# Waits between GpSimd and VectorE, and constant products in TensorE's early idle time, in a recurrent-attention and gated-MLP kernel

## The chip, the cores and the metric

The kernel runs on one core of a Trainium2 chip. The metric is the device time of one execution in microseconds; the time of a kernel is the median of its runs. The profile is of one execution. Its span goes from the first to the last instruction of the program; the execution's own time is a little longer.

The engines are named as in the profile: PE is TensorE's matmul, PEld its weight load, DVE is VectorE, ACT is ScalarE, POOL is GpSimd, and SP is the queue that issues DMAs. Each engine works through a list of instructions of its own.

## The reference

Two stages, in float32. First a recurrent attention with a decaying state, for 4 sequences, 8 heads, 768 steps, 48 values a head:

```python
for t in range(S):
    kt, vt, rt, wt = (k[:, :, t], v[:, :, t], r[:, :, t], w[:, :, t])
    cur = np.einsum('bhd,bhe->bhde', u[None] * kt, vt)
    y[:, :, t] = np.einsum('bhd,bhde->bhe', rt, state + cur)
    state = wt[:, :, :, None] * state + np.einsum('bhd,bhe->bhde', kt, vt)
```

Then an MLP on the 384 columns that the heads make together, with a gate that mixes the steps:

```python
h = x @ w_in                                  # 384 -> 1024
h = 0.5 * h * (1.0 + np.tanh(c * (h + 0.044715 * h ** 3)))
u, v = (h[..., :d_ff // 2], h[..., d_ff // 2:])
v_n = (v - mu) / np.sqrt(var + 1e-06) * g_ln  # mean and variance of v's 512 columns
v_s = np.einsum('ts,bsd->btd', w_sg, v_n) + b_sg[None, :, None]
return (x + (u * v_s) @ w_out).astype(np.float32)
```

## The kernel before

**The attention** goes in 24 chunks (4 sequences of 6 chunks of 128 steps), each in two halves of 64 steps. For a chunk the kernel loads the decays W, K and R together (KR), V (vtok) and, from the fifth chunk on, K and R by steps (RK). VectorE makes running products of the decays from both ends (L465 the suffix products, L473 or L480 the prefix products), multiplies K (L505) and R (L482) with them, TensorE makes the scores K R (L563), VectorE puts them into a masked matrix (L640), TensorE transposes K (L609), makes the products K V (L570), and the outputs from scores and state (L586, L597). The state is carried on by L654, L663, L670 and L683. The term with u needs `own`, a number for each step and head. For the first four chunks TensorE makes it from an elementwise K R (L515, then L519 against `u_col`). For the others it comes from RK: L527 multiplies by u, L529 by the other half, and L532 on VectorE sums.

**The MLP** works on float32 matrices that are split in two parts of reduced length, so that each product is three (L840, L841, L842). The weights come as float64 words and are split on the chip: L989, L991, L995 and L997 on VectorE for `w_in` (tile `vn`) and `w_out` (tile `g`), and for the first six, TensorE adds what is left (L1001 to L1003) and ScalarE copies it out. `w_sg` comes as float32 and is split by a copy (`wsgh`) and L1038 (`wsgl`). v's statistics are small 128x1 operations (tile `st`, L865 to L873), among them a power on GpSimd (L871).

**The order.** All this is written as some hundred small generators. Each yields an `Op` with the engines that could take it and a cost on each; `Plan.run` places the ops one after another by readiness and rank, picks an engine for each, and then lets the generator write the instructions. So the order of every engine's instructions comes from the costs in the plan, not from the chip. The plan treats some operations as users of a port that VectorE and GpSimd share:

```python
def port(self, e):
    return e == "POOL" or e == "DVE" and self.two
```

and plans no two of them at the same time. That is a matter of the plan alone: on the chip an instruction waits only for its data, its buffers, and its own engine.

**What the steps touch.** `m_m` is the pool of PSUM buffers for TensorE's products (tiles `m_ps`, three of them, and later `resets`). `full`, a 128x128 matrix of ones in `junk`, is set early on by GpSimd; `ident` is the unit matrix in the tile `same`, which GpSimd writes as the last of its preparations. `e_own`, `rk` and the like are the events and buffers by which the plan strings ops together. The transfers are issued on SP's queue in the plan's order: a load that waits for its buffer holds up those behind it.

Of the kernel before, what the change touches and what calls it, by code (L numbers as in the profile page):

```python
# [45 lines left out]
               (0, "load_v"): -15.0}  # L46
COLD = 15.0
FETCH = (3.6, 32, 66)
STRETCH = 6
RESETS = 8  # L50
AHEAD = {"decays": -0.24, "decayed_k": -1.91, "own_weights": 0.42, "masked": 0.16, "state": -0.26, "decayed": 1.33,
# [46 lines left out]
class Event:  # L98
    t = None
# [36 lines left out]
class Plan:  # L136
# [4 lines left out]
    def __init__(self):  # L141
        self.engines = dict.fromkeys(("PE", "DVE", "ACT", "POOL", "SP"), 0.0)
        self.procs = []
        self.log = []
        self.dma = 0.0
        self.lanes = [0.0] * 8
        self.port = 0.0
        self.count = 0
        self.pe_last = self.pe_before = None
        self.pos, self.came = FETCH[2], [0.0, 0.0]  # L150

    def fetched(self, t, end, n):

# [30 lines left out]
    def run(self):  # L184
        while True:
            best = {}
            for p in self.procs:
                op = p[3]
                if any(e.t is None for e in op.after) or any(len(s.free) < op.take.count(s) for s in op.take):
                    continue  # L190
                ready = max([p[2]] + [e.t for e in op.after] + [s.since(op.take.count(s)) for s in op.take])
                _, t, e = min((s + self.cost(op, e, s) + BIAS.get(e, 0.0), s, e) for e in op.on
                              for s in (max(ready, self.engines[e], self.port if op.port(e) else 0.0,
                                        self.lanes[0] if op.kb is not None else 0.0),))
# [9 lines left out]
            t, e, p = pick  # L204
            op = p[3]
            op.e, op.end = e, t + self.cost(op, e, t)
            if e == "PE":
                op.end += self.fetched(t, op.end, op.n)
            self.engines[e] = op.end
            if e == "PE":  # L210
                self.pe_before, self.pe_last = self.pe_last, op
# [6 lines left out]
            else:  # L218
                op.seen = op.end + self.LAT.get(e, 0.2)
            op.got = [s.take() for s in op.take]  # L220
            for b in op.free:
                b.done(op.seen)
            if op.done is not None:
                op.done.t = op.seen
            if not op.apart:
                p[2] = op.seen
            self.log.append((t, op.end, e, p[0], p[1].__name__))
            self._next(p, op)
            if p[3] is None:
                self.procs.remove(p)  # L230
        assert not self.procs, [(p[0], p[1].__name__) for p in self.procs[:40]]
# [70 lines left out]
def rwkv_gmlp(ctx: ExitStack, tc: tile.TileContext, wpad, kr, vtok, ktok, vt, u, ucol, w_in, consts_, w_sgT, w_out, out):  # L302
    nc = tc.nc
# [101 lines left out]
    plan = Plan()  # L405
    plan.engines.update(DVE=2.0, POOL=3.5, ACT=2.1, SP=0.8)
    PLANS.append(plan)
    steps = [(b, g) for b in range(B) for g in range(NC)]
    N = len(steps)

# [97 lines left out]
    def own_weights(n):  # L508

        x = ch[n]  # L510
        if n < ON_PE["own"]:
            op = yield Op({"DVE": 0.6, "POOL": 1.25}, after=[x.e_KR], take=[s_rk], done=x.e_own, two=True)
            rk, = op.got
            t = rk.tile.rearrange("p a b -> p (a b)")[:, 0:NP * C]
            engine[op.e].tensor_tensor(t, x.K, x.R, ALU.mult)  # L515
            op = yield Op({"PE": 0.8}, small=True, after=[e_uc], take=[m_m], free=[rk], n=16)
            m, = op.got
            for p in range(NP):
                nc.tensor.matmul(m.tile[:, 0:H], t[:, p * C:(p + 1) * C], u_col[:, p], start=(p == 0),  # L519
                                 stop=(p == NP - 1))  # L520
            op = yield Op({"DVE": 0.15, "ACT": 0.2}, take=[s_own], free=[m])
            own, = op.got
            copy(op.e, own.tile, m.tile[:, 0:H])
        else:
            op = yield Op({"POOL": 1.05, "DVE": 0.48}, after=[x.e_RK, e_u], two=True)
            t = x.rk.tile
            engine[op.e].tensor_tensor(t[:, 0], t[:, 0], u_bc, ALU.mult)  # L527
            op = yield Op({"POOL": 1.05, "DVE": 0.48}, two=True)
            engine[op.e].tensor_tensor(t[:, 1], t[:, 1], t[:, 0], ALU.mult)  # L529
            op = yield Op({"DVE": 0.47}, free=[x.rk], take=[s_own])  # L530
            own, = op.got
            nc.vector.tensor_reduce(own.tile, t[:, 1].rearrange("p (h e) -> p h e", e=D), AX.X, ALU.add)  # L532
# [760 lines left out]
```

## Time and profile before

| | |
|---|---|
| median of 3 runs | 371.54 us (369.52 to 372.68) |
| the profiled execution | 372.92 us |
| its span | 371.2 us |
| mean granted clock of TensorE | 0.989 |
| PE busy | 345.1 us, 93% of the span, 4429 instructions |
| DVE busy | 284.7 us, 77%, 571 instructions |
| ACT busy | 199.6 us, 54%, 520 instructions |
| POOL busy | 103.3 us, 28%, 140 instructions |
| HBM over the span | 131 GB/s |

How to read it: a row of a timeline has the start in us from the span's start, the time in us, the engine, the line, the operation, what it writes and reads, and the number of instructions merged in the row. In square brackets is the idle time of the engine before it and what ended it. Matmuls of float32 data appear as two records each, and their ends are modelled, so neighbouring rows overlap a little. Where a range of the profile has a granted clock, it is the share of full speed that TensorE's clock was given.

### The profile page before, as it was taken

Reading aid. Unit: us, or ns where it says so; the run is one execution under the profiler, and the core shown is the slowest. Engines: PE = TensorE matmul, PEld = TensorE weight load, DVE = VectorE, ACT = ScalarE, POOL = GpSimd, SP = SyncE. Lnnn points to the kernel's source line nnn. Section 1 sums busy time; section 2 is a strip of 40 time slices with the busy share of each in tenths; the row PEclk is TensorE's granted clock in tenths of the full one; section 3 lists DMA queues with packets and bytes.
Section 4 is the critical chain, followed back from the end, with each engine's and each line's share of the span. In section 5 each row is a group of like instructions: output and inputs, shape, how many; then the busy total and the mean of one; then the engine's idle time right before and its main releaser. Section 6 shows DMA issues by size and latency. Waiting matters only on the chain.

```text
span 371.2 us, 10746 instructions
## 1 busy us (share of the span) xinstructions
PE 345.1 (93%) x4429; PEld 312.5 (84%) x4429; DVE 284.7 (77%) x571; ACT 199.6 (54%) x520; POOL 103.3 (28%) x140
## 2 busy tenths in 40 slices
PE   2899588899999999999999999999999999999991
PEld 2576367679999889989899988999999899999991
DVE  7997999999999999899999998545726354553350
ACT  2666567767644677687564577521256783521110
POOL 6221917045233564534122611121100120100000
PEclk9989999999999999999999999999999999999997
DMA  8889477542435826746346620120445431001002
GB/s 243 330 272 312 150 241 221 177 159 71 125 119 175 263 76 196 245 133 189 92 141 191 194 77 3 64 79 6 140 152 181 134 117 50 1 0 44 21 8 66
DMA packets 23432, 50.64 MB, mean 136 GB/s; under 512 B 3024, under 2 KB 11984, under 8 KB 23376
## 3 DMA queue, kind: packets, MB, share of 16 engines
q1 hardware_dynamic: 23376, 49.88, 42.2%
q8 instruction: 37, 0.61, 0.7%
q14 instruction: 19, 0.16, 0.1%
HBM read 43.97 MB, written 4.72 MB: 131 GB/s over the span
## 4 chain that ended last, share of the span: by engine, by line
PE 69%; DVE 22%; issue 3%; DMA 2%; ACT 2%; SPq 0%; DVEq 0%; ACTq 0%
PE m_ps L840 14%; PE m_ps L841 13%; PE m_ps L842 13%; PE resets L840 5%; PE resets L842 5%; PE resets L841 5%; PE a_ps L563 4%; PE y_ps L586 3%; PE y_ps L597 2%; DVE W L465 2%; PE y_ps L570 2%; DVE W L473 2%; DVE KR L505 2%; DVE a L640 1%; DMA W<-in_wpad 1%
## 5 line engine op out<-in xcount | busy, mean ns | idle before, releaser
L840 PE MATMUL m_ps<-wsgh,vn 128*128 128x384 f32 x144 | 49.4, 343 | 0.3 <-ACT u L896 0.3
L841 PE MATMUL m_ps<-wsgl,vn 128*128 128x384 f32 x144 | 48.4, 336 | 0.0
L842 PE MATMUL m_ps<-wsgh,vn 128*128 128x384 f32 x144 | 48.4, 336 | 0.0
L871 POOL TENSOR_TENSOR st<-st,mhalf 128x1 f32<-128x1 f32 x24 | 17.3, 721 | 76.4 <-DVE st L869 69.4
L491 ACT ACTIVATE junk<-W 128x1040 bf16<-128x1040 f32 x24 | 25.7, 1070 | 13.4 <-DVE W L480 5.2
L840 PEld LDWEIGHTS m_ps<-wsgh,vn 128*128 128x128 f32 x144 | 27.0, 188 | 1.6 <-ACT u L896 0.6
L840 PE MATMUL m_ps<-xT,winh 128*128 128x384 f32 x78 | 27.0, 346 | 0.6 <-ACT kt L309 0.6
L841 PEld LDWEIGHTS m_ps<-wsgl,vn 128*128 128x128 f32 x144 | 27.0, 188 | 0.5
L842 PEld LDWEIGHTS m_ps<-wsgh,vn 128*128 128x128 f32 x144 | 27.0, 187 | 0.0
L840 PE MATMUL m_ps<-g,wouth 128*128 128x384 f32 (+1 forms) x80 | 26.8, 335 | 0.0
L842 PE MATMUL m_ps<-g,woutl 128*128 128x384 f32 (+1 forms) x80 | 26.4, 330 | 0.0
L841 PE MATMUL m_ps<-g,wouth 128*128 128x384 f32 (+1 forms) x80 | 26.4, 330 | 0.0
L841 PE MATMUL m_ps<-xT,winh 128*128 128x384 f32 x78 | 26.2, 336 | 0.0
L842 PE MATMUL m_ps<-xT,winl 128*128 128x384 f32 x78 | 26.2, 336 | 0.0
L563 PE MATMUL a_ps<-KR 64*64 64x128 f32 (+1 forms) x768 | 22.9, 256 | 1.1 <-DVE S L654 1.0
L527 POOL TENSOR_TENSOR RK<-RK,flat 128x384 f32<-128x384 f32 x17 | 20.9, 1234 | 10.7 <-DVE resets L920 6.4
L922 ACT CAST g<-m_ps 128x384 fp32r<-128x384 f32 x24 | 11.4, 477 | 21.4 <-DVE m_ps L920 21.4
L586 PE MATMUL y_ps<-a,vtok 64*64 64x64 f32 x768 | 21.3, 224 | 1.1 <-DVE S L670 0.6
L842 PE MATMUL m_ps<-winh,xT 128*128 128x512 f32 x51 | 20.2, 396 | 2.3 <-ACT xT L309 2.3
L465 DVE TENSOR_TENSOR_SCAN W<-W,D 128x520 f32<-128x520 f32 x16 | 21.9, 1371 | 0.0
L586 PEld LDWEIGHTS y_ps<-a,vtok 64*64 64x64 f32 x768 | 16.1, 134 | 6.7 <-issue 3.6
L942 DVE TENSOR_TENSOR o<-m_ps,x 128x384 f32<-128x384 f32 (+1 forms) x20 | 10.4, 529 | 14.6 <-PE m_ps L842 10.3
(184 smaller groups left out, 1009.5 us busy)
## 6 DMA issues: line engine op xcount, KB each, us to landing
KR<-in_kr SPq DMA_DIRECT2D x24, 512.0 KB, 4.5
RK<-in_ktok SPq DMA_DIRECT2D x20, 384.0 KB, 3.6
W<-in_wpad SPq DMA_DIRECT2D x24, 260.5 KB, 3.0
vtok<-in_vtok SPq DMA_DIRECT2D x24, 192.0 KB, 3.4
out<-o SPq DMA_DIRECT2D x23, 192.0 KB, 1.9
vn<-in_w_in SPq DMA_DIRECT2D x6, 512.0 KB, 6.9
KR<-in_w_in SPq DMA_DIRECT2D x6, 512.0 KB, 4.3
g<-in_w_sgT SPq DMA_DIRECT2D x6, 384.0 KB, 5.4
```

The costliest lines, as they stand in the source:

```text
L465: nc.vector.tensor_tensor_scan(Suf[:, WL - 1:0:-1], W[:, WL - 1:0:-1], r_one if early else D1[:, WL - 1:0:-1], 0.0, ALU.mult, ALU.add)
L473: nc.vector.tensor_tensor_scan(W[:, at], W[:, at], r_two, 0.0, ALU.mult, ALU.add)
L491: nc.scalar.activation(junk.bitcast(BF16).rearrange("p (a x) -> p a x", a=2), both, AF.Square, accum_out=chk[:, n:n + 1])
L527: engine[op.e].tensor_tensor(t[:, 0], t[:, 0], u_bc, ALU.mult)
L563: nc.tensor.matmul(ps_[64 * c_:64 * c_ + 64, j, p * C:p * C + (2 * T if c_ < turn else T)], x.K[rows, at:at + T], r_, start=True, stop=True)
L586: m = nc.tensor.matmul(place(y, j, q, r, c_), x.V[64 * c_:64 * c_ + 64, h * D - up(p, j):h * D - up(p, j) + 64], x.a.tile[64 * c_:64 * c_ ...
L840: nc.tensor.matmul(ps, lh, rh, start=(i == 0), stop=False)
L841: nc.tensor.matmul(ps, lh, rl, start=False, stop=False)
L842: nc.tensor.matmul(ps, ll, rh, start=False, stop=(i == n - 1))
L871: nc.gpsimd.tensor_tensor(rstd, var, c.mhalf, ALU.pow)
L922: nc.scalar.copy(gh, ps)
L942: nc.vector.tensor_tensor(o.tile[:, 0:w], ps, h_.x.tile[:, i, at], ALU.add)
```

## The change

It has two parts.

**GpSimd waits.** When the plan has placed an op, `port_order` looks at what it wrote. For an op on VectorE it notes the last instruction and the planned end. For an op on GpSimd it adds, to the first instruction, a wait for the last VectorE op whose planned end is not later than this op's planned start. VectorE gets no wait for GpSimd.

**Constant products.** TensorE multiplies a 128x128 constant by itself into a part of an `m_ps` buffer that nobody reads: eleven times `full` before anything else; two times `ident` ahead of each of the four `own` products (L519); and, for each wait of TensorE of more than 0.4 us that the plan foresees before 80 us of its own time, as many as fit at 0.22 us each, if a buffer is free by the plan. The plan's clock for TensorE starts at 6.4 us, and the products take no time in it.

```diff
+WARM = (11, 80.0, 0.22)
...
+            gap = t - self.engines[e] if e == "PE" and t < WARM[1] else 0.0
             self.engines[e] = op.end
...
             op.got = [s.take() for s in op.take]
+            if gap > 0.4:
+                self.fill(t - gap, int((gap - 0.15) / WARM[2]))
...
+            n = self.traced()
             self._next(p, op)
+            self.behind(op, n, t)
...
+    def warm(on, n, ps_):
+
+        for _ in range(n):
+            nc.tensor.matmul(ps_[:, 0:128], on, on, start=True, stop=True)
+
+    def fill(t, n):
+
+        free = [x for at, x in m_m.free if at <= t]
+        if free:
+            warm(ident, n, free[0])
+
+    warm(full, WARM[0], m_m.free[0][1])
+    plan.fill = fill
+    plan.engines["PE"] = 6.4
...
+    def port_order(op, n, t):
+
+        ins = nc.cur_bb.bb.instructions[n:]
+        if op.e == "DVE":
+            last = [i for i in ins if i.engine == mybir.EngineType.DVE]
+            if last:
+                on_dve.append((op.end, last[-1]))
+        elif op.e == "POOL" and ins:
+            before = [i for end, i in on_dve if end <= t + 0.01]
+            if before:
+                tc.add_manual_dep(ins[0], before[-1].name, wait, reason="port order")
+
+    plan.traced, plan.behind = lambda: len(nc.cur_bb.bb.instructions), port_order
...
             op = yield Op({"PE": 0.8}, small=True, after=[e_uc], take=[m_m], free=[rk], n=16)
             m, = op.got
+            warm(ident, 2, m.tile)
```

In the built program the instructions of VectorE, ScalarE, SP and GpSimd stand in the same order as before, and TensorE's too, but for 40 constant products put in between. The line numbers of the changed file are higher by 40 or 41 in the main part: L1038 is L1079 there, L527 L568, L529 L570, L482 L522, L465 L505, L505 L545, L519 L560 and L1001 L1042. The constant products are L421.

GpSimd, before, from its first split of `w_sg` on; in brackets are the signals that each row waits for:

```order
L1038 TENSOR_TENSOR wsgl<-g_414,wsgh 128x2x384 [waits DMAHW1_49,Activation_49]
L865 TENSOR_SCALAR st_0_113<-st_0_113 128x1 [waits Activation_49]
L1038 TENSOR_TENSOR wsgl<-g_463,wsgh 128x2x384 [waits DMAHW3_49,Activation_49]
L527 TENSOR_TENSOR RK_0_88<-RK_0_88,flat 128x384 [waits DMAHW6_49,DMAHW1_49]
L529 TENSOR_TENSOR RK_0_88<-RK_0_88 128x384 [waits Pool_49]
L527 TENSOR_TENSOR RK_0_89<-RK_0_89,flat 128x384 [waits DMAHW7_49]
L529 TENSOR_TENSOR RK_0_89<-RK_0_89 128x384 [waits Pool_49]
```

and the same rows now:

```order
L1079 TENSOR_TENSOR wsgl<-g_446,wsgh 128x2x384 [waits DMAHW1_49,DVE_49,Activation_49]
L906 TENSOR_SCALAR st_0_113<-st_0_113 128x1 [waits DVE_49,Activation_49]
L1079 TENSOR_TENSOR wsgl<-g_495,wsgh 128x2x384 [waits DMAHW3_49,DVE_49,Activation_49]
L568 TENSOR_TENSOR RK_0_88<-RK_0_88,flat 128x384 [waits DMAHW6_49,DMAHW1_49,DVE_49]
L570 TENSOR_TENSOR RK_0_88<-RK_0_88 128x384 [waits DVE_49,Pool_49]
L568 TENSOR_TENSOR RK_0_89<-RK_0_89,flat 128x384 [waits DMAHW7_49,DVE_49]
L570 TENSOR_TENSOR RK_0_89<-RK_0_89 128x384 [waits DVE_49,Pool_49]
```

The rows stand as before; each now waits for VectorE (DVE_49) too. The values of that signal in the built program say for which operation. They are given by the line numbers of before: the first L1038 waits for VectorE's own L1038, the L865 for an L471 behind it, the second L1038 for the L482 at the top of the next piece, the first L527 for the first L471 in it, its L529 for the L505, the second L527 for the second L471, and its L529 for the L540.

VectorE's order from that L482 on, which is the same before and now (with the line numbers of before):

```order
L482 TENSOR_TENSOR KR_0_84<-KR_0_84,W_0_80 128x512
L465 SCALAR_TENSOR_TENSOR W_0_79<-W_0_79,resets 128x520
L471 RECIPROCAL resets<-W_0_79 128x4
L473 SCALAR_TENSOR_TENSOR W_0_79<-W_0_79,resets 128x260
L309 CAST winl<-m_ps_0_130 128x512
L505 TENSOR_TENSOR KR_0_81<-KR_0_81,W_0_79 128x512
L640 COPY_PREDICATED a_0_98<-mask,a_ps_0_128 128x512
L471 RECIPROCAL resets<-W_0_79 128x4
L473 SCALAR_TENSOR_TENSOR W_0_79<-W_0_79,resets 128x260
L532 TENSOR_REDUCE own_0_90<-RK_0_88 128x8
L309 COPY look_0_93<-y_ps_0_129 128x1
L482 TENSOR_TENSOR KR_0_81<-KR_0_81,W_0_79 128x512
```

`resets`, `a_ps`, `m_ps` and `y_ps` lie in PSUM, the rest in SBUF. Nothing moved here: the waits tie GpSimd to places in this order. The L540 follows the last row.

TensorE, before, from its start to the first of the `w_in` products:

```order
L519 MATMUL m_ps_0_130<-u_col,RK_0_88 128x8 x3
L609 MATMUL m_ps_0_131<-same,KR_0_81 128x128 [waits DMAHW1_49,Pool_49]
L609 MATMUL m_ps_0_131<-same,KR_0_81 128x128 x3
L519 MATMUL m_ps_0_132<-u_col,RK_0_89 128x8 [waits DVE_49]
L519 MATMUL m_ps_0_132<-u_col,RK_0_89 128x8 x3
L563 MATMUL a_ps_0_128<-KR_0_81 64x64 [waits DVE_49]
L563 MATMUL a_ps_0_128<-KR_0_81 64x64 x15
L609 MATMUL m_ps_0_131<-same,KR_0_82 128x128 [waits DMAHW4_49,DVE_49,Activation_49]
L609 MATMUL m_ps_0_131<-same,KR_0_82 128x128 x3
L1001 MATMUL m_ps_0_130<-vn_184,same 128x512 [waits DVE_49,Activation_49]
```

and now, from the L609 of the first chunk on:

```order
L650 MATMUL m_ps_0_131<-same,KR_0_81 128x128 x3
L421 MATMUL m_ps_0_132<-same 128x128 x2
L560 MATMUL m_ps_0_132<-u_col,RK_0_89 128x8 [waits DVE_49]
L560 MATMUL m_ps_0_132<-u_col,RK_0_89 128x8 x3
L604 MATMUL a_ps_0_128<-KR_0_81 64x64 [waits DVE_49]
L604 MATMUL a_ps_0_128<-KR_0_81 64x64 x15
L650 MATMUL m_ps_0_131<-same,KR_0_82 128x128 [waits DMAHW4_49,DVE_49,Activation_49]
L650 MATMUL m_ps_0_131<-same,KR_0_82 128x128 x3
L421 MATMUL m_ps_0_132<-same 128x128 [waits Activation_49]
L421 MATMUL m_ps_0_132<-same 128x128 x9
L1042 MATMUL m_ps_0_130<-vn_195,same 128x512 [waits DVE_49]
```

Two constant products stand ahead of the second `own` product, and ten between the second transposes and the first of the `w_in` products; sixteen more stand ahead of everything shown, and twelve come later: two ahead of each `own` product of the third and fourth chunk, then one, two and five in waits that the plan foresees.

More of the change, by code (lines that the diff above doesn't have):

```diff
@@ L150, in __init__ @@
         self.pos, self.came = FETCH[2], [0.0, 0.0]
+        self.fill = lambda t, n: None
+        self.behind = lambda op, n, t: None
+        self.traced = lambda: 0
     def fetched(self, t, end, n):
@@ L407, in rwkv_gmlp @@
     PLANS.append(plan)
+    def warm(on, n, ps_):
[8 more added lines that the diff above has]
+    plan.engines["PE"] = 6.4
+    wait = mybir.DependencyInfo(mybir.DependencyClass.Sync, mybir.DependencyReason.DATA)
+    on_dve = []
+    def port_order(op, n, t):
[9 more added lines that the diff above has]
+    plan.traced, plan.behind = lambda: len(nc.cur_bb.bb.instructions), port_order
     steps = [(b, g) for b in range(B) for g in range(NC)]
```

## The prediction

> **What bounds the kernel now.** I read the busy time of each engine by stage first, and cut the stages where the picture changes.
>
> ```profile
> 0.00:12.40 12.40, 5.67 (x52) 5.15 (x52) 9.66 (x21) 3.56 (x8) 7.31 (x32) 1.00 0.85 279
> 12.40:38.90 26.50, 24.22 (x390) 16.20 (x390) 24.27 (x49) 18.46 (x51) 7.05 (x9) 0.94 0.86 294
> 38.90:94.90 56.00, 48.12 (x662) 38.56 (x661) 55.79 (x106) 38.21 (x97) 25.01 (x28) 1.00 0.52 160
> 94.90:360.90 266.00, 264.76 (x3316) 250.42 (x3317) 193.72 (x396) 139.41 (x365) 63.97 (x73) 1.00 0.36 112
> ```
>
> The columns are the stretch, its length, busy us of PE, PEld, DVE, ACT and POOL, the granted clock, the DMA share and GB/s. From 94.9 us on PE is never idle for long (1.24 us of 266), so a faster VectorE is worth nothing there. From 38.9 to 94.9 VectorE is busy 55.79 of 56 us and PE is idle for 7.88 us: VectorE bounds that stage, and what it saves there PE can take, up to those 7.88 us. Before 38.9 both are nearly full, PE partly at half clock.
>
> Next I read VectorE's timeline for rows longer than other rows of the same line.
>
> ```profile
> 12.40 1.72 DVE L989 TENSOR_SCALAR vn<-vn 128x512 int32<-128x512 int32 x2
> 17.73 0.40 DVE L989 TENSOR_SCALAR vn<-vn 128x512 int32<-128x512 int32 x1
> 19.15 0.68 DVE L991 SCALAR_TENSOR_TENSOR vn<-vn,vn 128x512 int32<-128x512 int32 x1
> 20.02 0.42 DVE L995 TENSOR_SCALAR vn<-vn 128x512 int32<-128x512 int32 x1
> 22.93 0.68 DVE L997 SCALAR_TENSOR_TENSOR winl<-vn,vn 128x512 fp32r<-128x512 uint32 x1
> 25.41 0.35 DVE L663 TENSOR_TENSOR S<-S,pc 128x192 f32<-128x192 f32 x1
> ...
> 36.80 0.72 DVE L640 COPY_PREDICATED a<-mask,a_ps 128x512 f32<-128x512 uint8 x1
> 38.96 2.04 DVE L989 TENSOR_SCALAR vn<-vn 128x512 int32<-128x512 int32 x1
> 41.19 1.22 DVE L991 SCALAR_TENSOR_TENSOR vn<-vn,vn 128x512 int32<-128x512 int32 x1
> 42.33 1.14 DVE L663 TENSOR_TENSOR S<-S,pc 128x192 f32<-128x192 f32 x1
> 43.40 1.22 DVE L995 TENSOR_SCALAR vn<-vn 128x512 int32<-128x512 int32 x1
> 44.81 1.22 DVE L997 SCALAR_TENSOR_TENSOR winl<-vn,vn 128x512 fp32r<-128x512 uint32 x1
> 46.55 1.22 DVE L465 TENSOR_TENSOR_SCAN W<-W,resets 128x520 f32<-128x520 f32 x1
> 49.22 0.68 DVE L505 TENSOR_TENSOR KR<-KR,W 128x512 f32<-128x512 f32 x1
> ...
> 58.80 1.82 DVE L873 TENSOR_TENSOR st<-st 128x1 f32<-128x1 f32 x1
> 63.50 0.83 DVE L663 TENSOR_TENSOR S<-S,pc 128x192 f32<-128x192 f32 x1
> 64.25 1.48 DVE L882 TENSOR_TENSOR vn<-v,vn 128x512 fp32r<-128x512 f32 x1
> 66.59 0.68 DVE L882 TENSOR_TENSOR vn<-v,vn 128x512 fp32r<-128x512 f32 x1
> 72.03 0.15 DVE L873 TENSOR_TENSOR st<-st 128x1 f32<-128x1 f32 x1
> 75.44 0.54 DVE L1010 TENSOR_TENSOR woutl<-g 128x384 fp32r<-128x384 f32 x1
> 79.94 1.19 DVE L1010 TENSOR_TENSOR woutl<-g 128x384 fp32r<-128x384 f32 x1
> 92.59 0.98 DVE L873 TENSOR_TENSOR st<-st 128x1 f32<-128x1 f32 x1
> ```
>
> And GpSimd's timeline at the same moments.
>
> ```profile
> 12.56 1.28 POOL L482 TENSOR_TENSOR KR<-KR,W 128x512 f32<-128x512 f32 x1 [0.73 <-DVE W L473]
> 36.87 1.84 POOL L1038 TENSOR_TENSOR wsgl<-g,wsgh 128x768 fp32r<-128x768 f32 x1 [0.84 <-ACT wsgh L309]
> 38.87 1.85 POOL L1038 TENSOR_TENSOR wsgl<-g,wsgh 128x768 fp32r<-128x768 f32 x1
> 40.68 1.18 POOL L527 TENSOR_TENSOR RK<-RK,flat 128x384 f32<-128x384 f32 x1
> ...
> 88.33 3.24 POOL L869 TENSOR_SCALAR st<-st 128x1 f32<-128x1 f32 x1 [2.88 <-ACT junk L867]
> ```
>
> L989 takes 0.40 us alone and 2.04 us when it starts 0.09 us behind a 1.85 us GpSimd operation: it waits until that one is done. L991 at 41.19 ends at 42.41, which is its 0.68 us behind the L527 of GpSimd that ends at 41.86; the long rows after it each find the next RK product of GpSimd in their way. L640 at 36.80 reads its values from PSUM and ends at 37.52, while GpSimd's L1038 runs on to 38.71: it is not held up. The Trainium skill, "SBUF — State Buffer", section "Who interferes with whom", says the same: a VectorE operation with two SBUF inputs, or in a two-port mode, and a GpSimd operation that reads SBUF exclude each other, and the first to start keeps the port.
>
> **What the waits are worth.** They keep GpSimd from running ahead of the planned order, so that each of its long operations falls behind the VectorE operation that the plan put ahead of it, which is mostly followed by one that reads PSUM. The excess of the long rows, each against its short row: 1.0 us at 12.40 (the pair took 1.72, two apart overlapping 0.08 would take 0.72), then 1.64, 0.54, 0.79, 0.80, 0.54 and 1.67 up to 60.6 us (6.0 in all), then 0.48, 0.80, 0.65 and 0.83 (2.8).
>
> What comes back: the L482 of GpSimd (12.56) now waits for L997, which ended at 17.2 us, and stands beside L640 (0.72) and for some 0.6 us against the L989 behind it; net 0.4. The L1038 of 38.87 now waits for VectorE's L482, whose successor starts at 46.55; from there to L505 at 49.22 nothing reads two SBUF inputs, 2.67 us, in which 1.85 us fit. The L527 behind it starts at about 48.5, lasts about 1 us and meets L505: 0.5 back. The second L527 meets the next VectorE L482 (0.3), an L871 at 58 us another (0.3): net 4.9 of 6.0. For 62 to 95 us I take 0.4 back: net 2.4. VectorE's sum is 0.4 + 4.9 + 2.4 = 7.7 us. From 95 us on the same kind of saving lies under PE and counts as zero; its cover is PE's 264.76 us of work, and if PE ever waited there the saving would count for more, not less.
>
> What is queued behind a waiting GpSimd operation is GpSimd's own order. The four L527/L529 end at about 54.2 us on the old clock, just ahead of the L532 on VectorE that reads the last of them; I bound this at 0 to 0.3 us each time. L482 of GpSimd also frees the buffer of the fourth W load, and SP's queue has a vn load right behind it:
>
> ```profile
> 17.53 0.37 SPq L984 DMA_DIRECT2D vn<-in_w_in  x1
> 27.49 0.40 DVE L989 TENSOR_SCALAR vn<-vn 128x512 int32<-128x512 int32 x1
> vn<-in_w_in SPq DMA_DIRECT2D x6, 512.0 KB, 6.9
> ```
>
> Both move by about 1.5 us (GpSimd's end at 17.2 + 1.3 against 17.05). With the median of 6.9 us from issue to landing, the vn load is there at 25.9, and VectorE reads it at 27.49. So SP costs nothing.
>
> **What the constant matmuls cost and bring.** PE rows:
>
> ```profile
> 9.55 1.88 PE L519 MATMUL m_ps<-u_col,RK 128*128 128x8 f32 x8 [0.15 <-DVE RK L515]
> 14.87 2.04 PE L1001 MATMUL m_ps<-vn,same 128*128 128x512 f32 x2 [1.33 <-DVE vn L991]
> 21.51 1.95 PE L519 MATMUL m_ps<-u_col,RK 128*128 128x8 f32 x16
> 29.70 0.29 DVE L309 COPY y<-y_ps 128x128 f32<-128x128 f32 x1 [1.82 <-ACT x L309]
> 43.49 0.51 PE L842 MATMUL m_ps<-winh,xT 128*128 128x512 f32 x1 [2.30 <-ACT xT L309]
> 27.00:28.00 1.00, 1.00 (x10) 0.67 (x11) 0.89 (x2) 0.79 (x2) 0.33 (x1) 0.50 0.92 353
> ```
>
> No row has a plain 128x128 float32 product. By L519, which loads the same weights and has two records each, one costs 1.95/8 = 0.24 us at full clock and 1.88/4 = 0.47 at half; more columns cannot be cheaper, so I take 0.25 and 0.47 as the ends. The first eleven and the five behind them (16 x 0.47 = 7.5 us at most) lie in the 6.7 us that PE is idle in the first stage and run about 1 us into L519, whose own eight records then take about half: nothing lost. The ten ahead of the first L1001 cost 2.5 us warm against a wait that was 1.33 us with PE cold, and PE arrives there earlier when warm: nothing again, but 4.7 us if cold. The four ahead of the L519 group at 21.51 stand on PE's path: 1.0 us. What they bring is the clock: it was 0.50 from 25 to 28.5 us, and behind that VectorE sat idle for 1.82 us. At full clock the 3.4 us of work shrink by 1.7; less 1.0 for the four, 0.7 to 0.8 us net; bounds -1.0 (clock falls anyway) and +1.8 (the whole wait). I take +0.8, since the fall follows weight loads with hardly any product, and the four break that up. The five at 40.6 us lay in a wait of 2.30 us which ended on ScalarE's xT behind VectorE's late L991; with that gone they stand exposed, 1.2 us less 0.2: minus 1.0 on PE.
>
> The row at 27 us shows PE busy for the whole microsecond at half clock. The Trainium skill, "TensorE: Matmul & The Clock Gate", Part 1, has the clock fall after an idle window of about 3.4 us; the trace differs, since PE was busy when it fell. By the page's rule the four products would do nothing for the clock, and the sum would be 1.8 us worse.
>
> **The sum.** VectorE could be 7.7 + 0.8 = 8.5 us earlier at 95 us. PE has to follow with the same work: it can give its 7.88 us of idle time and 0.8 of clock, less 1.0 for the exposed five. Of the idle time I leave a quarter, 1.9 us, standing: a choice, because waits on ScalarE stay and handovers get tighter. So 7.9 - 1.9 - 1.0 + 0.8 = 5.8 us. The profiled execution took 372.92 us (span 371.2), 1.38 above the median of 371.54; 372.92 - 5.8 = 367.1 there, 365.7 for a median.
>
> **Rivals.** *PE has no room.* Once VectorE stops waiting, PE between 38.9 and 94.9 is 86% full in an order that is fixed, and half of its idle time stays. For it: windows where both are full. Against: the longest wait, 2.30 us, hangs on rows that shrink. Gain 2.5, so 369.0.
>
> *The products run cold.* If the clock falls before 13.5 us, the ten take 4.7 us, L1001 starts at 18.2 instead of 14.9, and VectorE stands still behind the products that follow on PE, 3.3 us less some slack, say 2.7; with another 1.0 at 21.5 the gain falls to 2: 369.5. Against: sixteen back to back just before.
>
> *GpSimd starves (the slower side).* VectorE's next operation starts at once, GpSimd's only after the signal; if VectorE reads SBUF pairs back to back, GpSimd gets nothing, as at 88.33, where 128x1 took 3.24 us. Place: the RK products ahead of an L532, three times before 95 us (46, 68, 92), and the L871 ahead of an L873 twice (72, 81). At 3.24 less some 0.2 for the work, five times, VectorE would stand for 15.2 us against 7.7 gained: 7.5 us net, 379.0. It decides against the change as soon as VectorE's waits for GpSimd before 95 us come to more than the 7.7. Against: the operation behind the awaited one mostly reads PSUM.
>
> *The waits bind nothing*: where the awaited operation is long done nothing changes, 371.5. Against: from 38.87 on they bind for 7 us and more.
>
> **Chances.** Forecast 0.55; no room 0.18; cold 0.10; binds nothing 0.04; starved 0.13. Within 1%, what a measurement can tell from no change, is 367.8 to 375.3; so faster 0.56, same 0.31, slower 0.13. The range goes from 362.5 (all idle time gone) to 372.0 and leaves out the starved case and a little below.
>
> **What would show it.** Right: L989, L991, L663, L995 and L997 at about 40 us back to 0.4, 0.7, 0.35, 0.4 and 0.7 us; L873 at 0.15; GpSimd's L1038 and L527 7 us later in VectorE's order; PE without the wait of 2.30 us; full clock before 10 us and through 25 to 28.5; PE full from 89 instead of 95 us. Wrong: VectorE waiting for POOL RK or st, PE idle shared out anew, or L1001 later than 15 us.

## The result, and the profile after

The changed kernel takes 360.97 us (median; 359.32 to 362.9) where the kernel before, beside it on the same chip, takes 372.3 (369.52 to 373.5): a ratio of 0.9705, 95% interval 0.9661 to 0.9748. Once more on another chip the ratio was 0.9737 (0.9705 to 0.9769). The gain is 10 to 11 us, about twice the 5.8 that were forecast, and 360.97 lies below the range. The profiled execution took 360.7 us (span 359.0). In the changed kernel every line of before stands 40 or 41 further down (L989 is L1030), and L421 is the constant product.

Busy time by stage of the changed kernel, in the columns of the prediction. VectorE and PE are some 8.4 us ahead at the end of the third stretch, so I cut there; the end of the last is moved by the 12.2 us of the whole span, of which PE's work has won 10.3, so it holds a little less of that work than before:

```profile
0.00:12.40 12.40, 9.45 (x88) 9.04 (x88) 8.77 (x18) 3.46 (x8) 7.30 (x32) 0.97 0.83 293
12.40:38.90 26.50, 26.20 (x471) 20.19 (x464) 25.82 (x54) 19.26 (x53) 7.10 (x9) 0.95 0.87 291
38.90:86.50 47.60, 47.23 (x625) 38.92 (x624) 47.26 (x104) 37.63 (x96) 17.39 (x26) 1.00 0.58 186
86.50:348.70 262.20, 261.96 (x3304) 248.16 (x3304) 188.84 (x394) 138.57 (x365) 56.03 (x74) 1.00 0.37 114
```

The third stretch lasted 56.00 us before and PE was idle for 7.88 of them. Now it lasts 47.60, PE is idle for 0.37 and VectorE for 0.34: both are full, PE with 1.27 us of constant products among its work. From 86.5 us on PE is idle for 0.24 us, where it was 1.24.

VectorE's timeline, the rows that were long:

```profile
37.91 0.40 DVE L1030 TENSOR_SCALAR vn<-vn 128x512 int32<-128x512 int32 x1
38.49 0.68 DVE L1032 SCALAR_TENSOR_TENSOR vn<-vn,vn 128x512 int32<-128x512 int32 x1
39.09 0.35 DVE L704 TENSOR_TENSOR S<-S,pc 128x192 f32<-128x192 f32 x1
39.36 0.42 DVE L1036 TENSOR_SCALAR vn<-vn 128x512 int32<-128x512 int32 x1
39.96 0.68 DVE L1038 SCALAR_TENSOR_TENSOR winl<-vn,vn 128x512 fp32r<-128x512 uint32 x1
...
54.08 0.15 DVE L914 TENSOR_TENSOR st<-st 128x1 f32<-128x1 f32 x1
...
57.51 0.68 DVE L923 TENSOR_TENSOR vn<-v,vn 128x512 fp32r<-128x512 f32 x1
```

and GpSimd's beside it:

```profile
35.96 1.84 POOL L1079 TENSOR_TENSOR wsgl<-g,wsgh 128x768 fp32r<-128x768 f32 x1 [0.99 <-ACT wsgh L318]
37.77 0.24 POOL L906 TENSOR_SCALAR st<-st 128x1 f32<-128x1 f32 x1
41.38 1.86 POOL L1079 TENSOR_TENSOR wsgl<-g,wsgh 128x768 fp32r<-128x768 f32 x1 [3.38 <-ACT y L318]
43.20 1.00 POOL L568 TENSOR_TENSOR RK<-RK,flat 128x384 f32<-128x384 f32 x1
44.90 1.00 POOL L570 TENSOR_TENSOR RK<-RK 128x384 f32<-128x384 f32 x1 [0.69 <-DVE KR L545]
```

The second wsgl product no longer follows the first. GpSimd waits for 3.38 us. (The row puts the end of this wait down to ScalarE's y; by the signals of the built program the product waits for VectorE's L522 as well, the L482 of before, which starts at 40.56 us and ends at 41.24, 0.14 us ahead of it.) So VectorE has the whole split of vn and the L704 in its midst (2.04, 1.22, 1.14, 1.22 and 1.22 us before) to itself at 0.40, 0.68, 0.35, 0.42 and 0.68, and L914 (L873 before) is back from 1.82 to 0.15. Neither engine pays: GpSimd's own rows shorten too, as the groups of before and after show:

```profile
L527 POOL TENSOR_TENSOR RK<-RK,flat 128x384 f32<-128x384 f32 x17 | 20.9, 1234 | 10.7 <-DVE resets L920 6.4 <-DMA RK<-in_ktok 3.6 <-DVE S L663 0.7
```

```profile
L568 POOL TENSOR_TENSOR RK<-RK,flat 128x384 f32<-128x384 f32 x17 | 17.1, 1011 | 34.0 <-DVE RK L570 5.8 <-DVE W L520 5.1 <-DVE st L906 4.5
```

What PE waited for in 38.9 to 94.9 us of the kernel before (us in total, times, longest):

```profile
PE m_ps L842 <- ACT xT L309: 2.3, 1, 2.3
PE a_ps L563 <- DVE S L654: 1.0, 1, 1.0
PE m_ps L1003 <- DVE winl L997: 1.0, 1, 1.0
PE m_ps L609 <- DVE KR L505: 1.0, 1, 1.0
PE y_ps L597 <- DVE look L309: 0.7, 1, 0.7
PE m_ps L840 <- ACT kt L309: 0.6, 1, 0.6
PE m_ps L840 <- ACT v L863: 0.5, 1, 0.5
PE y_ps L597 <- POOL wsgl L1038: 0.3, 1, 0.3
PE a_ps L570 <- DVE a L640: 0.3, 1, 0.3
```

Three of them are put down to ScalarE, and each of these hangs on VectorE one step further back. ScalarE's xT, for which PE waited longest, stood behind a copy that had itself waited for VectorE's late L991. These are ScalarE's rows before:

```profile
42.44 0.62 ACT L1014 CAST winh<-vn 128x512 fp32r<-128x512 f32 x1 [1.56 <-DVE vn L991]
42.96 0.47 ACT L309 CAST xT<-m_ps 128x384 fp32r<-128x384 f32 x1
```

In the changed kernel the copy starts at 39.73 us without a wait and xT at 40.25. The v at 71.71 us follows a copy that waited 1.00 us for a VectorE split (L991 of `w_out`), and the kt at 81.95 follows an L876 that waited 0.96 us for VectorE's L873.

And from 38.9 us to the end in the changed kernel:

```profile
PE a_ps L611 <- DVE a L681: 0.2, 1, 0.2
```

That is the whole list of the waits it shows there; its second profile shows three of 0.3 us from the same place on. The chain that ended last says the same, first of before, then of after:

```profile
PE 69%; DVE 22%; issue 3%; DMA 2%; ACT 2%; SPq 0%; DVEq 0%; ACTq 0%
```

```profile
PE 89%; DVE 4%; DMA 3%; ACT 1%; SPq 1%; issue 0%; DVEq 0%
```

**The leads.** To see where time is won I subtract, for an instruction at the same place in an engine's list, its start in a variant from its start in the kernel before. The table, worked out so from the timelines, holds the changed kernel (twice, one execution each) and the variants that are told of below. The column heads are the place in time of the kernel before; V is VectorE, P is PE.

```
                      V 38   P 41   V 48   P 50   V 96   P 95   P 179  P 340
changed kernel        1.1    0.0    5.4    5.1    8.8    8.4    10.2   10.3
the same, again       2.5    1.5    6.8    6.5    9.9    9.6    11.4   11.6
waits only            1.3    1.3    5.6    5.4    9.0    8.7     9.4    9.5
products only         0.8   -0.3    0.7    0.7    0.7    0.7    -0.8   -0.8
waits up to 92 us     0.8   -0.3    5.1    4.8    7.6    7.3     6.6    6.6
waits from 92 us     -0.6   -0.6   -0.6   -0.6   -0.6   -0.6     0.8    0.9
without the five      2.5    2.5    6.8    6.6    8.7    8.4    10.2   10.3
five waits            2.0    1.4    6.4    5.1    5.5    5.5     5.7    5.7
the four only         1.8    1.3    6.2    5.0    8.8    8.4    10.2    8.8
```

VectorE is 8.8 us ahead at 96 us, and PE 8.4. Of these, 1.1 us (2.5 in the second profile) were there at 38 us, and that part is not shown to come from the change: the variants with waits from 92 us on and with five waits change nothing ahead of 38 us and stand at -0.6 and 2.0 there. From 38 to 95 us PE wins 7.3 and 7.1 us, nearly all of the 7.88 that it idled, not three quarters. Past 95 us it wins another 1.9 and 2.0. Of the profiled span's 12.2 us, 10.3 are these, and the other 1.9 lie in the last stores: one of them took 4.38 us from issue to landing in the profile of before, and the same store 2.04 in the changed kernel's.

### The profile page after: what moved, and what is told of

Its sections match the earlier page's. It is cut to its first block, busy times and chain, and to the rows that moved or that the text cites. A ratio compares the mean times of both kernels' runs of the same rounds, so it can differ in the third digit from the quotient of the medians.

```text
span 359.0 us, 10952 instructions
## 1 busy us (share of the span) xinstructions
PE 349.1 (97%) x4509; PEld 320.4 (89%) x4509; DVE 272.6 (76%) x571; ACT 198.9 (55%) x520; POOL 87.8 (24%) x140
## 4 chain that ended last, share of the span: by engine, by line
PE 89%; DVE 4%; DMA 3%; ACT 1%; SPq 1%; issue 0%; DVEq 0%
PE m_ps L881 17%; PE m_ps L883 16%; PE m_ps L882 16%; PE resets L881 6%; PE resets L883 5%; PE resets L882 5%; PE a_ps L604 5%; PE y_ps L627 4%; PE y_ps L638 3%; PE y_ps L611 2%; DMA W<-in_wpad 2%; PE m_ps L1042 2%; PE m_ps L421 2%; DMA x<-y 1%; PE m_ps L870 1%; PE m_ps L650 1%
## 5 line engine op out<-in xcount | busy, mean ns | idle before, releaser
L883 PE MATMUL m_ps<-wsgh,vn 128*128 128x384 f32 x144 | 48.4, 336 | 0.0
L912 POOL TENSOR_TENSOR st<-st,mhalf 128x1 f32<-128x1 f32 x24 | 13.3, 553 | 72.0 <-DVE st L910 37.7
L883 PEld LDWEIGHTS m_ps<-wsgh,vn 128*128 128x128 f32 x144 | 27.0, 188 | 0.0
L883 PE MATMUL m_ps<-g,woutl 128*128 128x384 f32 (+1 forms) x80 | 26.4, 330 | 0.0
L883 PE MATMUL m_ps<-xT,winl 128*128 128x384 f32 x78 | 26.2, 336 | 0.0
L568 POOL TENSOR_TENSOR RK<-RK,flat 128x384 f32<-128x384 f32 x17 | 17.1, 1011 | 34.0 <-DVE RK L570 5.8
L881 PE MATMUL m_ps<-winh,xT 128*128 128x512 f32 x51 | 21.1, 414 | 0.0
L959 DVE SCALAR_TENSOR_TENSOR m_ps<-m_ps,flat 128x384 f32<-128x384 f32 x24 | 14.8, 619 | 7.9 <-PE m_ps L883 7.8
L937 ACT ACTIVATE u<-m_ps 128x384 f32<-128x384 f32 x26 | 12.5, 490 | 14.5 <-PE m_ps L883 14.5
```

The source lines that it names most:

```text
L881: nc.tensor.matmul(ps, lh, rh, start=(i == 0), stop=False)
L883: nc.tensor.matmul(ps, ll, rh, start=False, stop=(i == n - 1))
L912: nc.gpsimd.tensor_tensor(rstd, var, c.mhalf, ALU.pow)
L937: nc.scalar.activation(h_.u[f].tile, ps, AF.Gelu_apprx_tanh)
L959: nc.vector.scalar_tensor_tensor(ps, ps, c.g[:, d:d + 1], c.b_bc[:, ts], ALU.mult, ALU.add)
```

## The experiments

My theory, formed from these two traces: the waits alone carry the gain, PE gives all of its idle time because every wait of it hung on VectorE, and the products are worth nothing. Rivals: the products carry part of it through the clock; or the prediction's own steps hold and something outside them gave the rest.

### The waits alone

```diff
     def warm(on, n, ps_):
-        for _ in range(n):
+        for _ in range(0):
             nc.tensor.matmul(ps_[:, 0:128], on, on, start=True, stop=True)
```

> GpSimd's waits alone, without any constant product; the outputs are the same. By the prediction's own steps: PE gives 6.0 of its 7.88 us of idle time between 38.9 and 94.9 us, nothing after, no clock gained and no five products to pay: 372.3 - 6.0 = 366.3 us. By the theory formed from the trace of the changed kernel, that PE gives all of its idle time there (7.9) and the short waits past 95 us too (1.5), the waits alone are worth 9.4 us: 362.9, about 2 above the full change, and most of that difference is the stretch at half clock before 28.5 us. Rival, that the constant products carry most of the gain through the clock: under 5 us gained, above 367.

Measured: 361.43 us against 370.92 before, ratio 0.9723 (0.9679 to 0.9767). That is the changed kernel's ratio within what can be told apart (some 1.6 us), and 3.5 us below what the prediction's steps give from the kernel before on this chip (370.92 - 6.0 = 364.9; the 366.3 above started from 372.3). The products are not needed for the gain. In the table its leads run with the changed kernel's from 48 us on. Without products in its row, PE's idle time in the stretch that was 38.9 to 94.9 us before falls from 7.88 to 1.08 us, and the stretch gets 7.4 us shorter:

```profile
37.60:86.20 48.60, 47.52 (x662) 38.70 (x662) 48.26 (x107) 38.37 (x97) 17.56 (x27) 1.00 0.57 182
```

It lost 0.95 us once, at 121 us of its own time, to a new wait on GpSimd:

```profile
121.15 0.50 PE L883 MATMUL resets<-winh,xT 128*128 128x512 f32 x1 [0.95 <-POOL xT L876]
```

### The constant products alone

```diff
-    plan.traced, plan.behind = lambda: len(nc.cur_bb.bb.instructions), port_order
```

> The constant products alone, GpSimd as before; the outputs are the same. Prediction's steps: the clock is full through 25 to 28.5 us (worth 0.8), the five at 40.6 us lie in the 2.30 us that PE waits there and cost nothing: 371.5. Theory from the trace of the changed kernel: the same, 1.1 us at most, 371.2. Rival, that the products carry the gain: more than 4 us, under 368. VectorE's L989, L991, L663, L995 and L997 near 40 us keep their long rows (2.0, 1.2, 1.1, 1.2, 1.2) in the first two cases.

Measured: 370.85 us against 370.92, ratio 0.9987 (0.9964 to 1.001): no gain that can be told, though the 0.8 us of the prediction lies inside the interval. The trace has PE 0.7 us ahead from 48 to 96 us, until a stall of 1.36 us at 156 us, which the profile ties to nothing, takes more than that. VectorE's long rows stay, and the five products lie in PE's wait, which shrinks from 2.30 to 1.17 us. The first row is of VectorE's timeline in this variant, the other two of PE's:

```profile
38.21 2.04 DVE L1029 TENSOR_SCALAR vn<-vn 128x512 int32<-128x512 int32 x1
```

```profile
39.84 1.27 PE L421 MATMUL m_ps<-same 128*128 128x128 f32 x10
...
42.75 0.50 PE L882 MATMUL m_ps<-winh,xT 128*128 128x512 f32 x1 [1.17 <-ACT xT L318]
```

### Waits up to 92 us, and waits from 92 us on

Two variants that split the waits at GpSimd's 37th planned operation, the RK product at 92 us. The first keeps the products, the second has none.

```diff
         elif op.e == "POOL" and ins:
+            on_pool.append(op)
             before = [i for end, i in on_dve if end <= t + 0.01]
-            if before:
+            if before and len(on_pool) <= 37:
```

> The constant products, and the waits only for the first 37 operations of GpSimd (up to the RK product at 92 us of the kernel before); those behind run as before. Outputs are the same. Prediction's steps (past 95 us everything lies under PE and counts as zero): as the full change, 361.0. Theory from the trace of the changed kernel (the short PE waits past 95 us go as well): PE is about 8.7 us ahead at 106 us and gains no more: 362.5, 1.5 behind the full change. Bounds: with the late conflicts back VectorE could fall behind PE again and give some back, at worst 364.

```diff
-            if before:
+            if before and len(on_pool) > 37:
```

> No constant products, and waits only for GpSimd's operations behind the 37th, so nothing is changed before 92 us. Outputs are the same. Prediction's steps: zero, 372.3. Theory from the trace of the changed kernel: PE idles only 1.24 us from 94.9 us on, so at most 1.2 to 1.5 us are gained: 370.9 to 371.1, and VectorE's lead past 95 us grows by more than PE's. Rival, that waits past 95 us make room for more than PE's own idle time shows: under 370.

Measured: the early waits 363.7 us, ratio 0.9794 (0.9745 to 0.9843); the late ones 370.35, ratio 0.9977 (0.9947 to 1.0006). The late waits bring 0.9 us by the ratio (0.6 by the medians), with zero in the interval, and leaving them out costs some 2 to 3 us against the changed kernel, where the intervals touch. So the times alone do not settle their worth. The traces say more. Without the late waits PE's lead falls from 7.3 to 6.6 past 95 us instead of rising by 1.9; with them alone it rises by 1.5, from -0.6 to 0.9, and these are PE's waits of before past 95 us:

```profile
PE y_ps L586 <- DVE S L670: 0.6, 1, 0.6
PE resets L842 <- DVE vn L882: 0.3, 1, 0.3
PE m_ps L840 <- ACT u L896: 0.3, 1, 0.3
```

and all that the late waits leave of them:

```profile
PE m_ps L882 <- ACT u L938: 0.3, 1, 0.3
```

In the traces, then, 1.5 us are won where the prediction counted zero. One execution each is thin for it: in the early variant PE also lost 0.8 us at 149 us to "issue", a wait that the profile ties to nothing.

### Without the five products at 40 us

```diff
-            warm(ident, n, free[0])
+            warm(ident, n if n != 5 else 0, free[0])
```

> The full change without the five constant products at 40 us; outputs the same. By the prediction's steps they stand exposed: 1.0 us less than the full change, 360.0, and PE reaches the L840 behind them 1.0 us sooner. If PE is full from there on, as the trace of the changed kernel shows, that 1.0 stays to the end. Rival, that VectorE sets the pace there (42.76 of 43.10 us busy): the same time as the full change, and PE waits for what it gained. The waits alone, with no product at all, came to 361.4 on a chip with 370.9 for the kernel before, which speaks for the rival.

Measured: 360.84 us, ratio 0.9732 (0.9699 to 0.9765), beside 360.41 and 0.9737 of the changed kernel on that chip: the same. PE does reach L840 at 41 us with a lead of 2.5 instead of 1.5, and then waits for what it gained:

```profile
38.08 0.40 PE L881 MATMUL m_ps<-winh,xT 128*128 128x512 f32 x1
38.32 0.40 PE L882 MATMUL m_ps<-winl,xT 128*128 128x512 f32 x1
39.52 0.50 PE L883 MATMUL m_ps<-winh,xT 128*128 128x512 f32 x1 [0.81 <-ACT xT L318]
```

In the changed kernel the five stand there instead, and L883 follows without a wait:

```profile
39.51 1.27 PE L421 MATMUL m_ps<-same 128*128 128x128 f32 x10
40.54 0.48 PE L881 MATMUL m_ps<-winh,xT 128*128 128x512 f32 x1
40.86 0.40 PE L882 MATMUL m_ps<-winl,xT 128*128 128x512 f32 x1
41.10 0.39 PE L883 MATMUL m_ps<-winh,xT 128*128 128x512 f32 x1
```

So PE's row without a gap was partly filled with work that nothing waited for. The five did not cost the 1.0 us that the prediction booked: at 50 us PE's lead is 6.6 without them and 6.5 with them. (The times alone, each some 1.2 us uncertain, would not rule it out.)

### Five waits only

```diff
-            if before:
+            if before and 10 < len(on_pool) <= 15:
```

> No constant products, and waits for five GpSimd operations only: the second L1038 at 38.87 us and the two pairs L527/L529 behind it. Outputs the same. VectorE's excess that this takes away: L989 1.64, L991 0.54, L663 0.79, L995 0.80, L997 0.54, 4.3 us, less 0.8 for meetings further on: 3.5 to 4.3 us for VectorE by 55 us in every theory. Prediction's conversion (three quarters of what PE idles): a gain of 2.6 to 3.2, 367.7 to 368.3. PE gives all of it: 3.5 to 4.3, 366.6 to 367.4. Both against 370.9; the lead of PE in the trace against VectorE's decides more sharply than the time.

Measured: 368.04 us against 370.77, ratio 0.9928 (0.9904 to 0.9952), a gain of 2.7 (1.8 to 3.6). By the time, the three quarters of the prediction (2.6 to 3.2) fit better than the whole (3.5 to 4.3), whose lower end just lies in the interval. The traces speak for the whole, from one execution each: VectorE comes to 5.5 us at 96 us from 2.0 at 38, PE to 5.5 from 1.4 at 41. From 66 us on the two leads are equal within 0.1 us. What VectorE gives, PE takes here, as far as it has waits. (The 2.0 us at 38 come from the clock in this execution and not from the waits; see below. VectorE's own saving by the five waits is 3.5: it was 4.3 at 48 us, and 0.9 was given back in meetings further on.) PE's wait at L842 is nearly halved and not gone: xT comes 2.5 us earlier, but PE itself comes 1.4 us earlier too:

```profile
40.97 0.50 PE L884 MATMUL m_ps<-winh,xT 128*128 128x512 f32 x1 [1.22 <-ACT xT L318]
```

### The waits with four products

```diff
-        for _ in range(n):
+        for _ in range(n if n == 2 and len(on_dve) > 20 else 0):
```

with the planner's fills and the first eleven left out, so that the two pairs ahead of the L519 group are all.

> All the waits, and of the constant products only the four ahead of the L519 group at 21.5 us; outputs the same. Prediction's steps: the four cost 1.0 and bring a full clock worth 1.8 through 25 to 28.5 us, so 0.8 less than the waits alone: 360.6. Rival, that the clock falls anyway: 1.0 more than the waits alone, 362.4. Third, that neither shows at the end since VectorE is the later one there: 361.4. The clock rows of 22 to 29 us tell the first two apart.

Measured: 361.15 us, ratio 0.9743 (0.9712 to 0.9774): the third case, neither cost nor gain shows, within some 1.2 us. The clock was full in its profile up to the last 5 us.

### The changed kernel again

> The changed kernel once more, beside the variants below and on their chip. Every theory: a ratio of 0.9705 within 0.004, some 361 us. Its last out transfers show whether the tail of the profile before (4.38 us for the longest) belongs to a kernel or to one execution: if to one execution, the longest here lies anywhere from 1.9 to 4.4 us.

Measured: 360.41 us, ratio 0.9737 (0.9705 to 0.9769). The longest of its last stores took 2.2 us, so the 4.38 us are not the kernel's before: the variant with five waits had one of 4.32 us as well, and of the others' that were recorded none took more than 3.2.

### Extra work on PE and on VectorE

If PE is full and VectorE is full, which of them sets the pace? Four variants add known work. On PE ten constant products, ahead of an L840 group at some 60 us of the plan, once in the kernel before and once in the changed one; on VectorE fourteen small reciprocals on a tile of their own, in the changed kernel, at 60 us and at 110 us of the plan.

```diff
+    def pe_probe(op, t):
+        free = [x for a, x in m_m.free if a <= t]
+        if op.e == "PE" and t >= 60 and free and not probes:
+            probes.append(t)
+            for _ in range(10):
+                nc.tensor.matmul(free[0][:, 0:128], ident, ident, start=True, stop=True)
```

```diff
+    def ve_probe(op, t):
+        if op.e == "DVE" and t >= 60 and not probes:      # 110 in the other
+            probes.append(t)
+            nc.vector.memset(spare, 1.0)
+            for _ in range(14):
+                nc.vector.reciprocal(spare, spare)
```

> The kernel before (no waits, no products) with ten constant products at one place, ahead of the L840 group of the third FFN step that the plan puts at some 60 us. At 0.25 us each, 2.5 us of extra PE work. Outputs the same. If VectorE alone bounds that stage and PE's idle time there is slack, they cost 0 to 0.5: PE idles 0.71 + 0.53 + 0.64 + 0.29 us in its longer waits from 65 to 95 us and more in short ones. If PE and VectorE hand over to each other so tightly that work on either delays both, up to 2.5.

> The changed kernel with the same ten products at the same place. PE shows no wait there, so if PE is the bound they cost 2.5 us in full. If VectorE sets the pace, as the variant without the five products suggests (no gain from 1.0 us less on PE), they cost clearly less: 1.5 or below, and VectorE shows no new wait for PE.

> The changed kernel with a small VectorE operation of its own (one fill of 128x8 and fourteen reciprocals of 128x8 in place, at 0.12 to 0.18 us each, 1.7 to 2.7 us) put in at some 60 us by the plan. Outputs the same. If VectorE still bounds there, they cost what they last, 1.7 to 2.7 us; if PE alone is the bound from 40 us on, VectorE has 0.3 us of slack in that stage and they cost the rest too, since 42.76 of 43.10 us are taken: so both give 1.5 or more here, and only a much looser VectorE (under 0.8) would contradict both.

> The same VectorE work put in at some 110 us by the plan, where PE shows no wait and VectorE is busy for 112.7 of 118 us from 82 to 200 us. If PE alone bounds there, the 5.3 us in which VectorE is idle swallow it: 0 to 0.5. If PE waits for VectorE at once whenever VectorE is late, 1.5 or more. The prediction took the first: VectorE's time past 95 us counts as zero.

Measured, against 371.23 us before on that chip: the PE load in the kernel before 371.99, ratio 1.0024 (1.0 to 1.0048); in the changed kernel 361.7, ratio 0.9772 (0.9736 to 0.9809); the VectorE load at 60 us 365.79, ratio 0.9875 (0.984 to 0.991), and at 110 us 365.46, ratio 0.984 (0.9795 to 0.9884). The loads themselves, of the changed kernel's two variants (PE's timeline, then VectorE's):

```profile
59.32 2.39 PE L455 MATMUL m_ps<-same 128*128 128x128 f32 x20
```

```profile
60.26 3.29 DVE L456 RECIPROCAL spare<-spare 128x8 f32<-128x8 f32 x14
```

The 2.39 us on PE cost 0.8 us (0 to 1.8) in the kernel before. In the changed one they cost 1.3 us by the ratios (0.9772 less 0.9737, times 371; some 2 us uncertain), and 1.9 by the leads at 340 us (9.4 against 11.6, less 0.4 that stood at 66 us already, ahead of the load). The load on VectorE came to 3.3 us, longer than the 1.7 to 2.7 that were expected. It cost 5.1 and 3.8 us by the ratios, each some 2 us uncertain. At once PE shows waits, first in the variant at 60 us, then at 110:

```profile
65.97 0.66 PE L665 MATMUL m_ps<-same,KR 128*128 128x128 f32 x4 [1.54 <-ACT xT L318]
...
68.08 0.50 PE L896 MATMUL m_ps<-winh,xT 128*128 128x512 f32 x1 [0.93 <-ACT v L919]
```

```profile
116.18 0.70 PE L642 MATMUL y_ps<-a,vtok 64*64 64x64 f32 x16 [2.46 <-DVE S L726]
```

The leads say what of this is the load. In the variant at 60 us VectorE's falls by 3.3 us across the load (7.7 to 4.4), and at 95 us PE's is 5.3 where the changed kernel's is 8.4: some 3 us. The rest of the 5.1 us was not taken apart. In the variant at 110 us PE loses 2.5 us against the changed kernel at the wait shown, and 1.6 more right behind it, because the granted clock is at 0.50 from 116.2 to 119.6 us. GpSimd, which waits for VectorE's operations by the change, is held up too (its next RK product starts at 114.1 us, 5.1 us behind the one before); what that cost was not taken apart. The six executions of this variant fall into two groups: three with a mean granted clock of 0.997 or 0.998 took 362.7 to 364.8 us, three with 0.989 to 0.992 took 366.2 to 366.9, and the profiled one is of the second. Against the changed kernel on that chip (0.9737 of 371.23, so 361.5) the first group paid 1.2 to 3.3 us.

So in the changed kernel work on either engine is paid: VectorE's in full at 60 us and for a good part at 110 us, where a fall of the clock can come on top, and PE's, by the leads of one execution, for half or more. VectorE's slack past 95 us is small: 5.3 us of idle time in 82 to 200 us did not take in 3.3 us of work.

## Why the prediction was wrong, point by point

- **VectorE bounds 38.9 to 94.9 us, by 55.79 of 56 us; GpSimd's operations in its way are the cause.** Right. The waits alone give the whole gain, and the five longest rows of the split fall to the 0.4, 0.7, 0.35, 0.4 and 0.7 us that were named.
- **VectorE's sum: 7.7 by the waits, 8.5 with the clock, at 95 us.** Right for the waits: 8.8 in the changed kernel, of which 1.1 were there at 38 us. From 38 to 96 us it won 7.7 (7.4 again, and 7.8 with the waits alone) where 4.9 and 2.4 were forecast.
- **"Of the idle time I leave a quarter, 1.9 us, standing: a choice, because waits on ScalarE stay and handovers get tighter."** This is the step that failed. The quarter did not stand: from 38 to 95 us PE wins 7.1 to 7.4 us of the 7.88 (changed kernel twice, waits alone), where the prediction let it take 6.0. The waits "on ScalarE", 2.30, 0.64 and 0.53 us, were waits on VectorE at one remove: ScalarE's xT stood behind a copy that VectorE's late split held up, and the wait went with the split. In the variant with five waits PE follows VectorE within 0.1 us from 66 us on.
- **"From 95 us on the same kind of saving lies under PE and counts as zero."** The second failure, of the same kind: PE's 1.24 us there were left out as short, and PE wins 1.9 us past 95 in the changed kernel, 1.5 with the late waits alone, 0.8 with all waits and no products, where a new wait on GpSimd took 0.95 back. By the times this is 0.9 to 3 us and not settled.
- **The five products at 40 us, minus 1.0.** Wrong: leaving them out gains nothing that can be told, for PE then waits 0.81 us for ScalarE's xT in their place.
- **The ten ahead of L1001: nothing if warm; L1001 at 18.2 us if cold.** Between the two. In the first profile they took 3.17 us, with the clock at 0.50 up to 15.0 us, and L1042 (L1001 before) started at 16.42 instead of 14.87, later than the 15 us that were named as a sign of being wrong; at 17.9 us PE had made that up. In the second profile they took 2.40 us and it started at 13.5.

```profile
13.42 3.17 PE L421 MATMUL m_ps<-same 128*128 128x128 f32 x20
16.42 1.02 PE L1042 MATMUL m_ps<-vn,same 128*128 128x512 f32 x2
```

- **The clock: four products cost 1.0 and bring 1.8 by a full clock through 25 to 28.5 us.** Not shown. In the changed kernel's profile the stretch at half clock did not go, it came earlier (the first row; the second is the stretch that had half clock before):

```profile
11.60:15.00 3.40, 3.40 (x44) 3.28 (x45) 3.30 (x9) 1.66 (x6) 1.05 (x1) 0.50 1.03 410
...
25.10:28.50 3.40, 3.40 (x59) 2.31 (x59) 3.20 (x8) 3.38 (x13) 0.51 (x1) 1.00 0.87 273
```

With five waits and no product at all it did not fall ahead of the last 6 us:

```profile
25.10:28.50 3.40, 3.40 (x60) 2.42 (x59) 3.37 (x10) 3.15 (x11) 0.82 (x1) 1.00 0.82 251
```

A full clock is worth about what was said, 1.8 us: in that profile VectorE's lead went from 0.2 us at 27 to 2.0 at 32. So the products neither kept it from falling in every execution nor were needed for that. They may make the fall rarer: the mean granted clock was 0.995 to 0.999 in all twelve executions with the products alone, and 0.985 to 0.996 in the 23 of the kernel before beside them. That mean also holds the half clock of the last microseconds, so it is no count of falls, and the times of the variants with and without products agree.
- **SP and the vn load: no cost.** Right: L1030 reads that load at 27.89 us against 27.49 before, without a wait.
- **Rivals.** *PE has no room* was the opposite of what happened. *The products run cold* happened in part, in one profile, and cost nothing at the end. *Binds nothing* fell with the waits alone. *GpSimd starves*: VectorE's waits for GpSimd are 0.8 and 0.7 us in all, as before. The slower GpSimd did reach PE once, in the waits alone, for 0.95 us.

With the failed terms put right the sum reads 7.9 + 1.5 + 0 + 0 = 9.4 us in place of 7.9 - 1.9 - 1.0 + 0.8 = 5.8. The first interval allows 9.4 to 12.6 us (0.9748 and 0.9661 of 372.3), the second 8.6 to 10.9. What the 9.4 may still lack was not traced; the lead at 38 us (1.1 and 2.5) cannot be counted for it, since executions with nothing changed ahead of 38 us differ by as much (-0.6 and 2.0).

The Trainium skill, "SBUF — State Buffer", section "Who interferes with whom", has some operations of VectorE and GpSimd exclude each other on a shared port. The runs agree: an instruction waited for that port as well as for its data (L989 took 2.04 us before and 0.40 now), and with the order enforced, VectorE's busy time falls from 284.7 to 272.6 us and GpSimd's from 103.3 to 87.8 with the same operations. The Trainium skill, "TensorE: Matmul & The Clock Gate", Part 1, ties the fall of the clock to an idle window ahead of it; the kernel before differs, for its clock fell at 25.1 us behind 7.10 us in which PE was busy for 7.05:

```profile
18.00:25.10 7.10, 7.05 (x181) 5.67 (x182) 6.82 (x15) 3.75 (x14) 1.90 (x2) 1.00 0.88 285
```

## What to carry to other kernels

Where one engine bounds a stage, ask for each wait of the other what it hangs on two steps back: a wait that is put down to a third engine went with the bounding engine's delay, and nearly all of the idle time came back (7.1 to 7.4 of 7.88 us), not three quarters of it. Two operations that block each other on a port cost both engines (12.1 us of VectorE's busy time and 15.5 of GpSimd's here); a wait that makes one of them come later, where its result has time, gave some 10 us here and cost 0.95 us in one execution. An engine without gaps in its row is not proven to be the bound: taking the five products off PE gained nothing that can be told, and 3.3 us more work on VectorE at 60 us cost at least some 3.

## What the runs showed of the hardware that was not expected

- The clock's fall to 0.50 is a matter of the execution as much as of the kernel: the changed kernel had a stretch of about 3.4 us at half clock from 11.6 us on in one profile and none ahead of the last 3 us in another; the kernel before with the PE load at 65 us had one of about 6.8 us from 39.7 us on, and the changed one with the VectorE load at 110 us one of 3.4 us from 116.2 us on, right behind a PE wait of 2.46 us.
- PE stalls of 0.8 to 1.6 us that the profile ties to nothing ("issue") stood at different places in different variants: 0.8 at 149 us with the early waits, 1.36 at 156 us with the products alone, 1.43 at 199 us with the four products, 1.32 at 51 us without the five, 1.56 at 208 us in the kernel before with the PE load. Profiles of one execution differ by as much as a term of 1 us for that reason, and such terms are read from timed executions, or from leads, place by place.
- One store of 192 KB among the last took 4.3 to 4.4 us in two of the profiles (the kernel before and the five waits) and about 2 in most others.
